# A fused attention and spectral-mixing kernel: product with v moved inside the slot, last tokens of v by pair, constants on other engines

## The chip, the cores and the metric

The kernel runs on one core of a Trainium2 chip. The time is device time in microseconds of one execution; the runs shown are separate executions of the same program. The core has TensorE (in profiles PE, with its weight loads as PEld), VectorE (DVE), ScalarE (ACT), GpSimd (POOL) and SyncE (SP), which here only issues transfers. Each engine works off its own queue in order.

## The reference

Attention over 8 batches and 8 heads, 576 tokens of 64 values, with a causal window of 128 tokens and a linear penalty by distance; then a spectral mixing over the tokens with 64 modes and complex weights, and a residual with a ReLU.

```python
scores = scale * np.matmul(q, k.transpose(0, 1, 3, 2))
rel = pos[:, None] - pos[None, :]
bias = slopes[:, None, None] * (-np.abs(rel).astype(np.float32))[None, :, :]
mask = (rel >= 0) & (rel < window)
...
x = attention output, heads side by side          # (8, 576, 512)
X = np.fft.rfft(x, axis=1)                        # the first 64 modes are used
Yr = einsum('bmd,mde->bme', Xr, w_r) - einsum('bmd,mde->bme', Xi, w_i)
Yi = einsum('bmd,mde->bme', Xr, w_i) + einsum('bmd,mde->bme', Xi, w_r)
y = np.fft.irfft(Y, n=S, axis=1)
u = x + y
return u + np.maximum(u @ w_ch, 0.0)
```

The weights w_r and w_i are 64 matrices of 512 x 512 in float32 each, 134 MB together. Reading them is most of the traffic (163.6 MB are read in all).

## The kernel before

**Units and groups.** A unit is one pair of heads `s` of one batch `b`; there are N = 32. `GROUPS = ((0,), (1, 2, 3))` splits the pairs: units 0 to 7 are pair 0 of the eight batches, units 8 to 31 are pairs 1, 2, 3 of batch 0, then of batch 1, and so on. The rows of the weights that belong to pair 0 can be multiplied as soon as all of group 0 has its spectrum, which happens in the shadow of the attention of group 1. The rows of pairs 1 to 3 need all 32 units.

**Slots.** The instructions of the five engines are laid out by hand (`tc.manual_schedule`): each engine works in the order in which the Python code emits. `_slot(g, n, w0, w1)` (line 603) emits one step of a software pipeline: first half of the scores of unit n (`_score`, line 473), the transposes of q and k of unit n+1 (`_tr`) with their copies out of PSUM by ScalarE (`_evac`), the spectrum of unit n-2 (`_spectrum`, line 564: 5 matmuls for a unit of group 0; for group 1 it does nothing except at the last pair of a batch, where it issues 15), weight tiles of group 0 (`_modes`; one tile is three modes, 24 matmuls), the second half of the scores of unit n, the GpSimd casts of q and k of unit n+2 (`_cast_qk`) and of v of unit n+1 (`_cast_v`), the sorting of v's tokens into tiles of keys (`_keys`, line 432), the product of unit n-1 with v (`_av`, line 521), and a third of the mask product on GpSimd (`_mask3`). The PSUM tiles of scores, of the product with v and of the spectrum have one buffer each.

**Weight tiles in the slots.** From slot 10 on most slots carry one tile of group 0's weights in `w0`; slots whose spectrum has 15 matmuls carry none up to slot 18 and one later. Each tile's load is issued by SyncE at its slot and must wait until the tile three earlier is used: the pool `wpool` has `RING = 3` buffers for each of the tags `wr` and `wi`. All loads share SyncE's one queue, so a load that waits for a buffer holds up every load behind it. At most 8 transfers are under way at a time, since a new one waits for the one eight before it.

**The last 64 tokens of v.** They do not fill a tile of 128 and are handled apart. `_load_vt` (line 379) loads them for all batches and pairs with eight transfers of 128 KB, issued with unit 1, into the first buffers of the `wr` and `wi` rings; VectorE casts them to bfloat16 in two instructions (line 143); `_vt` (line 407) sorts them by a selector matrix `selt` on TensorE, four matmuls of 512 columns for a pair of heads, and VectorE copies the result to `vbt`. Pairs 0 and 3 are done after slot 0, pair 1 after slot 1, pair 2 after slot 2. The tile in PSUM is the single buffer `acc` that `_modes` uses later.

**Constants.** `_consts` (line 238) builds the matrix of the Fourier transform: angles on VectorE, then ScalarE's sine; and the distances for the masks on GpSimd (lines 287 to 295). `_mask` lets ScalarE take the exp of the distances: for pair 0 before slot 0, for pairs 1 to 3 after slot 2. `_select` (line 391) fills the selectors `sel` and `selt` on VectorE.

**Loads of q and k.** They come in batches of units: for group 0 the sizes are 1, 2, 3, 2 units, for group 1 three units each, three buffers in a ring.

After the last slot (n = 35, of which the last four carry no new unit) the weights of group 1 are streamed and multiplied (`_modes` with `last=True`), with the products of x and w_ch in between, and `_finish` makes the output.

Of the kernel before, what the change touches and what calls it, by code (L numbers as in the profile page):

```python
# [16 lines left out]
P = 128  # L17
# [4 lines left out]
ROWS = 3  # L22
# [12 lines left out]
def kernel(  # L35
# [27 lines left out]
    for j, grp in enumerate(GROUPS):  # L63
        mine = [n for n in range(N) if units[n][0] == j]
        sizes = [len(grp)] * B if len(grp) > 1 else [1, 2, 3, 2]
        for m in sizes:
            g.batch[mine[0]], mine = mine[:m], mine[m:]
# [28 lines left out]
    with tc.manual_schedule(engines={ET.SP, ET.PE, ET.Activation, ET.DVE, ET.Pool}):  # L96
        with ExitStack() as wctx:
# [4 lines left out]
            with ExitStack() as actx:  # L102
# [18 lines left out]
                with tc.tile_pool(name="tmpc", bufs=1, side="right") as tp:  # L121
                    for n in range(n0):
# [7 lines left out]
                        if n == 1:  # L130
                            _load_vt(g, tp)
# [9 lines left out]
                    _select(g, tp)  # L141
                    for i, t in enumerate(g.vtf):
                        nc.vector.tensor_copy(
                            g.vtb[:, 4 * i : 4 * i + 4].rearrange("p b c -> p (b c)"),
                            t[:, 0 : 16 * g.D])
                    first = list(dict.fromkeys(u[1] for u in units[:2]))
                    rest = [s for s in range(NP) if s not in first]
                    for s in first:
                        _mask(g, tp, s)
                    for n in range(3):  # L150
                        _slot(g, n, [], [])
                        for s in (first + rest)[n::3]:
                            _vt(g, s, nc.vector.tensor_copy)
                    for s in rest:
                        _mask(g, tp, s)
# [16 lines left out]
                for n in range(3, N + 2 + TAIL):  # L172
# [65 lines left out]
def _consts(g, tp):  # L238
    nc = g.nc
    NM, S, ST = g.NM, g.S, g.ST  # L240
    pi = tp.tile([P, 1], I32)
    nc.gpsimd.iota(pi, [[0, 1]], base=0, channel_multiplier=1)
    mi = tp.tile([P, 2, NM], I32)
    nc.gpsimd.iota(mi, [[0, 2], [1, NM]], base=0, channel_multiplier=0)
# [3 lines left out]
    make_identity(nc, g.ident_b)  # L248
# [3 lines left out]
    pcol = tp.tile([P, 1], FP32)  # L252
    nc.vector.tensor_copy(pcol, pi)
    mrow = tp.tile([P, 2, NM], FP32)
    nc.vector.tensor_copy(mrow, mi)
    scol = tp.tile([P, ST], FP32)
    for st in range(ST):
        nc.vector.tensor_scalar_add(scol[:, st : st + 1], pcol, float(st * P))
    nc.vector.tensor_scalar_add(scol[64:128, 4:5], pcol[64:128], float(4 * P - 64))
    phrow = tp.tile([P, 2, NM], FP32)  # L260
    nc.vector.memset(phrow[:, 0, :], S / 4.0)
    nc.vector.memset(phrow[:, 1, :], S / 2.0)
    MAGIC = float(2**23)
    ang = tp.tile([P, ST * P], FP32)
    for st in range(ST):
        nc.vector.scalar_tensor_tensor(
            out=ang[:, st * P : (st + 1) * P],
            in0=mrow.rearrange("p a b -> p (a b)"),
            scalar=scol[:, st : st + 1], op0=ALU.mult,
            in1=phrow.rearrange("p a b -> p (a b)"), op1=ALU.add,  # L270
        )
    kf = tp.tile([P, ST * P], FP32)
    nc.vector.tensor_scalar_mul(kf, ang, 1.0 / S)
    nc.vector.tensor_scalar(kf, kf, MAGIC, -MAGIC, op0=ALU.add, op1=ALU.add)
    nc.vector.scalar_tensor_tensor(
        out=ang, in0=kf, scalar=-float(S), op0=ALU.mult, in1=ang, op1=ALU.add)
    nc.scalar.activation(
        g.F.rearrange("p a b -> p (a b)"), ang, AF.Sin, scale=2.0 * math.pi / S)
# [4 lines left out]
    eng = nc.gpsimd  # L283
# [3 lines left out]
    eng.tensor_copy(rel, reli)  # L287
    eng.tensor_scalar_add(rel[64:128, 0:256], rel[64:128, 0:256], 127.0)
    eng.tensor_scalar_add(rel[64:128, 256:320], rel[64:128, 256:320], 64.0)
    eng.tensor_scalar(off, rel, 0.0, FAR, op0=ALU.is_lt, op1=ALU.mult)  # L290
    eng.tensor_tensor(out=rel, in0=rel, in1=off, op=ALU.add)
    eng.tensor_scalar(off, rel, float(P), FAR, op0=ALU.is_ge, op1=ALU.mult)
    for a, z, c in ((0, 256, 0), (0, 192, 256), (256, 320, 448)):
        eng.tensor_tensor(
            out=g.rel[:, c : c + z - a], in0=rel[:, a:z], in1=off[:, a:z], op=ALU.add)
    for vb in g.vbs:
        eng.memset(vb[:, :, :, g.D : g.D + 1], 1.0)
    eng.memset(g.vbt[:, :, :, g.D : g.D + 1], 1.0)
    eng.tensor_tensor(
        out=g.ident2, in0=g.ident_b[:, 0:64], in1=g.ident_b[:, 64:128], op=ALU.add)  # L300


def _mask(g, tp, s):
# [75 lines left out]
def _load_vt(g, tp):  # L379


    g.vtb = tp.tile([P, g.B, 4 * g.D], BF16, name="vtb")
    g.vtf = [g.wpool.tile([P, ROWS, g.DM], FP32, tag=tag, name=f"vt{tag}") for tag in ("wr", "wi")]
    g.vtf = [t.rearrange("p a e -> p (a e)") for t in g.vtf]
    for b in range(g.B):
        t = g.vtf[b // 4][:, 256 * (b % 4) : 256 * (b % 4) + 256]
        g.nc.sync.dma_start(
            out=t, in_=g.v[b, :, 512:576, :].rearrange("h (t r) d -> t h (r d)", r=4))


def _select(g, tp):
# [3 lines left out]
    nc.vector.memset(g.sel, 0.0)  # L395
    src = g.ident_b.rearrange("p (i u h) -> p i h u", i=2, h=2)
    for c in range(2):
        nc.vector.tensor_copy(g.sel[:, :, :, c, c::2], src)
# [204 lines left out]
def _slot(g, n, w0, w1):  # L603
# [9 lines left out]
    if 0 <= n - 2 < N:  # L613
        _spectrum(g, n - 2)
# [271 lines left out]
```

## Time and profile before

| | us |
|---|---|
| median of 3 runs | 472.33 |
| the runs | 470.13, 472.33, 472.79 |
| the profiled execution | 470.12 |
| its span, first to last instruction | 468.3 |
| first scores of slot 0, 1, 2, 3 | 7.35, 20.01, 25.41, 29.88 |
| first scores of slot 4, 5, 6, 8 | 35.35, 39.78, 43.97, 52.55 |
| first scores of slot 16, 24, 31 | 90.62, 130.25, 173.45 |
| last spectrum starts | 181.28 |
| last weight tile of group 0 done | 185.4 |

TensorE is busy for 72% of the span, the transfers' 16 engines for 95.3%, VectorE 49%, ScalarE 40%, GpSimd 31%. The shares are means over stages with different limits: attention until about 187 us, the stream of weights until about 430 us, the output after that. A timeline row gives start, duration, engine, line, operation, output and inputs, how many instructions are merged into the row, and in square brackets the idle time before it and what ended it. A row of a stretch gives, for each engine, busy time and instructions, then the granted clock of TensorE (1.00 or 0.50 here), the share of the 16 transfer engines in use, and what they moved in GB/s.

### The profile page before, as it was taken

To read this page: it belongs to the slowest core of one execution; us is meant where nothing else is said; L and a number is where in the kernel's file an instruction comes from. 1 tells how busy PE (TensorE), PEld (TensorE's weight loads), DVE (VectorE), ACT (ScalarE), POOL (GpSimd) and SP (SyncE) were. 2 spreads that over 40 slices of the span, in tenths; PEclk is the share of its full clock that TensorE was granted. 3 is DMA by queue.
4 is the path that set the end of the run, shared out by engine and by line. 5 is a ranking of instruction groups with operands and counts; after the bars stand their busy time and mean duration, and the time that the engine had idled before them with its cause. 6 is when DMAs were issued, how large, how long until landed. Compare 5 with 4: busy or idle time off the path is not lost.

```text
span 468.3 us, 13885 instructions
## 1 busy us (share of the span) xinstructions
PE 337.6 (72%) x5991; PEld 235.5 (50%) x6019; DVE 227.4 (49%) x454; ACT 188.0 (40%) x282; POOL 143.8 (31%) x186
## 2 busy tenths in 40 slices
PE   2788788987889986555666566565664668877994
PEld 1467677766678774333443333343333345634552
DVE  7568776758565564233233233232342334511884
ACT  6487765757555461113222022111220123301783
POOL 8468876759566432000000000000000000000783
PEclk9998997989865597557555565665755759978999
DMA  8999999999979987999999999999999999993687
GB/s 252 294 399 403 347 343 386 383 380 396 395 272 292 349 298 281 421 418 423 402 422 425 423 423 424 422 425 422 423 426 420 426 422 398 420 422 164 233 308 269
DMA packets 60317, 173.92 MB, mean 371 GB/s; under 512 B 4960, under 2 KB 14176, under 8 KB 60256
## 3 DMA queue, kind: packets, MB, share of 16 engines
q1 hardware_dynamic: 60256, 173.03, 95.3%
q8 instruction: 47, 0.77, 0.6%
q14 instruction: 14, 0.11, 0.1%
HBM read 163.58 MB, written 9.44 MB: 369 GB/s over the span
## 4 chain that ended last, share of the span: by engine, by line
DMA 39%; PE 25%; ACT 5%; DVE 4%; issue 3%; SPq 1%; POOL 1%; ACTq 0%; POOLq 0%; DVEq 0%
DMA wi<-in_moe_w_i_dram 38%; PE acc L682 4%; PE acc L678 3%; PE xt L588 2%; PE sc L488 2%; PE vps L444 2%; PE mm L713 2%; PE av L538 2%; PE xw L726 2%; ACT att L502 1%; PE tqk L460 1%; PE zwp L746 1%; PE tp L704 1%; PE y L713 1%; ACT hl L730 1%
## 5 line engine op out<-in xcount | busy, mean ns | idle before, releaser
L730 ACT CAST hl<-xw 64x512 bf16<-64x512 f32 x72 | 41.7, 579 | 165.4 <-PE xw L726 137.4
L682 PEld LDWEIGHTS <-wi 128*128 128x128 bf16 x1024 | 65.8, 105 | 72.6 <-DMA wi<-in_moe_w_i_dram 67.2
L852 POOL TENSOR_TENSOR o<-r,ys 128x512 f32<-128x512 f32 x18 | 22.5, 1273 | 249.9 <-ACT ys L843 249.8
L678 PEld LDWEIGHTS <-wr 128*128 128x128 bf16 x1024 | 69.7, 106 | 43.1 <-DMA wr<-in_moe_w_r_dram 25.6
L682 PE MATMUL acc<-Xlast,wi 128*128 128x16 bf16 x768 | 55.9, 193 | 49.0 <-DMA wi<-in_moe_w_i_dram 49.0
L731 DVE TENSOR_TENSOR hl<-xw,hl 64x512 bf16<-64x512 f32 x72 | 49.6, 689 | 83.3 <-ACT hl L730 83.2
L502 ACT ACTIVATE att<-sc 128x1024 bf16<-128x1024 f32 x64 | 65.5, 1023 | 56.6 <-PE sc L488 31.4
L678 PE MATMUL acc<-Xlast,wr 128*128 128x16 bf16 x768 | 63.0, 194 | 25.0 <-DMA wr<-in_moe_w_r_dram 19.9
L512 DVE TENSOR_TENSOR att<-att,mask 128x1024 bf16<-128x1024 bf16 x64 | 43.6, 683 | 43.4 <-ACT att L502 42.9
L517 POOL TENSOR_TENSOR att<-att,mask 128x512 bf16<-128x512 bf16 x32 | 44.5, 1390 | 51.1 <-ACT att L502 51.1
L726 PE MATMUL xw<-wch,xT 128*128 128x512 bf16 x121 | 54.0, 573 | 4.9 <-issue 3.1
L706 DVE COPY xT<-tp 128x512 bf16<-128x512 bf16 x36 | 15.2, 423 | 58.4 <-PE tp L704 58.2
L468 ACT COPY qkT<-tqk 128x576 bf16<-128x576 bf16 x62 | 39.3, 634 | 0.3 <-PE tqk L460 0.2
L460 PE MATMUL tqk<-ident_b,qkb 64*64 64x64 bf16 x1152 | 30.5, 209 | 9.9 <-ACT qkb L422 4.4
L488 PE MATMUL sc<-qkT,qkT 64*64 64x256 bf16 (+1 forms) x512 | 30.6, 313 | 9.6 <-ACT qkT L468 4.1
L460 PEld LDWEIGHTS <-qkb 64*64 64x64 bf16 x1152 | 30.2, 125 | 11.2 <-ACT qkb L422 4.6
L726 PEld LDWEIGHTS <-xT 128*128 128x128 bf16 x144 | 19.1, 138 | 22.3 <-issue 20.2
L444 PE MATMUL vps<-vc,sel 128*64 128x128 bf16 x512 | 25.5, 254 | 1.8 <-issue 0.7
L429 POOL CAST vc<-v 128x512 bf16<-128x512 f32 x32 | 26.1, 815 | 0.9 <-PE sc L497 0.9
L538 PE MATMUL av<-vb,att 128*128 128x65 bf16 x448 | 23.0, 211 | 0.6 <-DVE x L558 0.6
L555 DVE TENSOR_TENSOR x_sb<-av,rec 128x512 bf16<-128x512 f32 x32 | 22.1, 692 | 0.6
L678 PE MATMUL acc<-X,wr 128*128 128x16 bf16 x256 | 19.1, 193 | 4.2 <-ACT ZTa L691 4.2
(119 smaller groups left out, 526.8 us busy)
## 6 DMA issues: line engine op xcount, KB each, us to landing
wr<-in_moe_w_r_dram SPq DMA_DIRECT2D x85, 768.0 KB, 8.3
wi<-in_moe_w_i_dram SPq DMA_DIRECT2D x85, 768.0 KB, 9.7
v<-in_v_dram SPq DMA_DIRECT2D x64, 128.0 KB, 7.3
out_dram<-o SPq DMA_DIRECT2D x32, 256.0 KB, 2.3
q<-in_q_dram SPq DMA_DIRECT2D x9, 864.0 KB, 9.1
k<-in_k_dram SPq DMA_DIRECT2D x9, 864.0 KB, 10.1
q<-in_q_dram SPq DMA_DIRECT2D x2, 576.0 KB, 6.1
k<-in_k_dram SPq DMA_DIRECT2D x2, 576.0 KB, 7.3
```

The costliest lines, as they stand in the source:

```text
L444: g.nc.tensor.matmul(o[64 * r : 64 * r + 64, i, h], lhsT=g.sel[:, i, h, c], rhs=v[:, 2 * c + r], start=(c == 0), stop=(c == 1), tile_posit ...
L460: g.nc.tensor.transpose(tp[hs, r, :], u.b[w][hs, r], g.ident_b[hs, hs], tile_position=(64 * hh, 64 * hh))
L468: (copy or g.nc.scalar.copy)(dst.rearrange("c (p r) -> c p r", r=g.R), u.tp[w].rearrange("c r p -> c p r"))
L488: nc.tensor.matmul(sc[64 * r : 64 * r + 64, hh, c0 : c0 + nq], lhsT=kT[hs, kt * P + r : kt * P + P : 2], rhs=qT[hs, kt * P : kt * P + nq], ...
L502: nc.scalar.activation(a.rearrange("p h c -> p (h c)"), sc.rearrange("p h c -> p (h c)"), AF.Exp, scale=1.0 / math.sqrt(g.D))
L512: nc.vector.tensor_tensor(out=a, in0=a, in1=m, op=ALU.mult)
L517: g.nc.gpsimd.tensor_tensor(out=a, in0=a, in1=g.mask[:, g.units[n][1], :, 256:512], op=ALU.mult)
L678: nc.tensor.matmul(o, lhsT=wr[:, a].bitcast(BF16)[:, 1::2][:, c], rhs=X[:, a, 1:3, :, m], start=(a == 0), stop=False)
L682: nc.tensor.matmul(o, lhsT=wi[:, a].bitcast(BF16)[:, 1::2][:, c], rhs=X[:, a, 0:2, :, m], start=False, stop=(a == A - 1))
L726: nc.tensor.matmul(xw, lhsT=xT[:, dt], rhs=g.wch[:, dt], start=(dt == 0 and g.way[n] != "q"), stop=(dt == 3))
L730: nc.scalar.copy(g.hl[hi, n, h], xw[hi])
L731: nc.vector.tensor_tensor(out=g.hl[lo, n, h], in0=xw[hi], in1=g.hl[hi, n, h], op=ALU.subtract)
```

## The change

Six edits go together.

1. In `_slot` the product with v (`_av` of unit n-1) and the spectrum (of unit n-2) change places: the product now stands between the transposes and the second scores, the spectrum behind the keys.
2. The last tokens of v are loaded and sorted pair by pair. Pair 0 is loaded with unit 0 (two transfers of 128 KB) into a tile of its own; pairs 1 to 3 with six transfers ahead of the first weight tile, into one buffer of the `wr` ring. GpSimd casts one pair at a time, and TensorE sorts it with 64 matmuls of 64 columns (by batch, quarter and head of the pair). Pair 0 is done after slot 0, pairs 1, 2, 3 after slots 3, 4, 5, each with its mask ahead of it on ScalarE.
3. The distances are computed on VectorE, in place of GpSimd, with fewer instructions.
4. The chain of angles on VectorE is shorter.
5. The selectors are filled by GpSimd in place of VectorE.
6. The batches of q and k for group 0 are 1, 2, 2, 3 units.

```diff
-        sizes = [len(grp)] * B if len(grp) > 1 else [1, 2, 3, 2]
+        sizes = [len(grp)] * B if len(grp) > 1 else [1, 2, 2, 3]
...
-                        if n == 1:
-                            _load_vt(g, tp)
+                        if n == 0:
+                            for s in GROUPS[0]:
+                                _load_vt(g, s, tp.tile([P, 2, 4 * g.D], FP32, name=f"vtf{s}"))
+                        if n == g.first[1] - 1:
+                            t = g.wpool.tile([P, ROWS, DM], FP32, tag="wr", name="vtf")
+                            for i, s in enumerate(GROUPS[1]):
+                                _load_vt(g, s, t[:, i].rearrange("p (h c) -> p h c", h=2))
...
-                    _select(g, tp)
-                    for i, t in enumerate(g.vtf):
-                        nc.vector.tensor_copy(
-                            g.vtb[:, 4 * i : 4 * i + 4].rearrange("p b c -> p (b c)"),
-                            t[:, 0 : 16 * g.D])
...
+                    for s in GROUPS[0]:
+                        _mask(g, s)
+                    _select(g)
+                    todo_s = [(0, s) for s in GROUPS[0]] + [(3 + i, s) for i, s in enumerate(GROUPS[1])]
+                    for n in range(g.first[1] - 1):
                         _slot(g, n, [], [])
-                        for s in (first + rest)[n::3]:
-                            _vt(g, s, nc.vector.tensor_copy)
-                    for s in rest:
-                        _mask(g, tp, s)
+                        for k, s in todo_s:
+                            if k == n:
+                                if s not in GROUPS[0]:
+                                    _mask(g, s)
+                                _vt(g, tp, s)
...
+    prod = tp.tile([P, ST, NM], FP32)
+    nc.vector.tensor_tensor(
+        out=prod, in0=scol.unsqueeze(2).broadcast_to([P, ST, NM]),
+        in1=mrow.unsqueeze(1).broadcast_to([P, ST, NM]), op=ALU.mult)
+    ang = tp.tile([P, ST, 2, NM], FP32)
+    for ri in range(2):
+        nc.vector.tensor_scalar_add(ang[:, :, ri], prod, S / (4.0 - 2 * ri))
...
+    nc.vector.tensor_scalar(kf, ang, 1.0 / S, MAGIC, op0=ALU.mult, op1=ALU.add)
+    nc.vector.tensor_scalar(kf, kf, -MAGIC, -float(S), op0=ALU.add, op1=ALU.mult)
+    nc.vector.tensor_tensor(out=ang, in0=ang, in1=kf, op=ALU.add)
...
+    nc.vector.tensor_copy(rel[0:64], reli[0:64])
+    nc.vector.tensor_scalar_add(rel[64:128, 0:256], reli[64:128, 0:256], 127.0)
+    nc.vector.tensor_scalar_add(rel[64:128, 256:320], reli[64:128, 256:320], 64.0)
+    nc.vector.tensor_scalar(off, rel, 1.0 - P, FAR, op0=ALU.add, op1=ALU.mult)
+    nc.vector.scalar_tensor_tensor(
+        out=rel, in0=rel, scalar=-FAR, op0=ALU.mult, in1=rel, op1=ALU.max)
     for a, z, c in ((0, 256, 0), (0, 192, 256), (256, 320, 448)):
-        eng.tensor_tensor(
-            out=g.rel[:, c : c + z - a], in0=rel[:, a:z], in1=off[:, a:z], op=ALU.add)
+        nc.vector.tensor_tensor(
+            out=g.rel[:, c : c + z - a], in0=rel[:, a:z], in1=off[:, a:z], op=ALU.max)
...
+    g.selt = tp.tile([P, g.B, 4, 64], BF16, name="selt")
+    nc.gpsimd.memset(g.sel, 0.0)
+    nc.gpsimd.memset(g.selt, 0.0)
...
-def _load_vt(g, tp):
+def _load_vt(g, s, t):
+    for hh in range(2):
         g.nc.sync.dma_start(
-            out=t, in_=g.v[b, :, 512:576, :].rearrange("h (t r) d -> t h (r d)", r=4))
+            out=t[:, hh], in_=g.v[:, 2 * s + hh, 512:576, :].rearrange("b (t r) d -> t b (r d)", r=4))
+    g.unit["vt", s] = t
...
+def _select(g):
+    nc = g.nc
     src = g.ident_b.rearrange("p (i u h) -> p i h u", i=2, h=2)
     for c in range(2):
+        nc.gpsimd.tensor_copy(g.sel[:, :, :, c, c::2], src)
+    src = g.ident_b.rearrange("p (t b) -> p b t", b=g.B)
     for r in range(4):
+        nc.gpsimd.tensor_copy(g.selt[:, :, r, r::4], src)
...
+def _vt(g, tp, s):
+    nc = g.nc
+    v = tp.tile([P, 2, 4, g.D], BF16, tag="vtb", bufs=2, name=f"vtb{s}")
+    nc.gpsimd.tensor_copy(v.rearrange("p h r d -> p h (r d)"), g.unit.pop(("vt", s)))
     acc = g.mpsum.tile([P, 4, 2, MB, 8], FP32, tag="acc", name="vtp")
...
-    for r in range(4):
-        g.nc.tensor.matmul(acc, lhsT=g.selt[:, s, r], rhs=v[:, r], start=(r == 0), stop=(r == 3))
-    copy(g.vbt[:, s, :, 0 : g.D], acc)
+    for b in range(g.B):
+        for r in range(4):
+            _pair(nc, acc[:, b], [g.selt[:, b, r]] * 2, [v[:, h, r] for h in range(2)],
+                  start=(r == 0), stop=(r == 3))
+    nc.vector.tensor_copy(g.vbt[:, s, :, 0 : g.D], acc)
...
         _tr(g, n + 1, 1)
-    if 0 <= n - 2 < N:
-        _spectrum(g, n - 2)
+    if 0 <= n - 1 < N:
+        _av(g, n - 1)
     for w in w0:
         _modes(g, *w)
...
         _keys(g, n)
-    if 0 <= n - 1 < N:
-        _av(g, n - 1)
+    if 0 <= n - 2 < N:
+        _spectrum(g, n - 2)
     if n < N:
         _mask3(g, n)
```

`_pair` (line 710, unchanged) issues two matmuls that fill the two halves of the output's partitions.

## The prediction

> **What bounds it now.** First the page: the slices (11.7 us each) and the chain of waits.
>
> ```profile
> span 468.3 us, 13885 instructions
> ...
> PEclk9998997989865597557555565665755759978999
> DMA  8999999999979987999999999999999999993687
> ...
> DMA 39%; PE 25%; ACT 5%; DVE 4%; issue 3%; SPq 1%; POOL 1%; ACTq 0%; POOLq 0%; DVEq 0%
> ```
>
> From slice 17 on (187 us) the transfers are full and the chain is almost all "wi": the three-pair weights are streamed, and nothing here touches that stream. It can begin only when the last spectrum is done and ring buffers come free. So the time is the end of the attention part (0 to 187 us) plus 283 us that stay, and I only ask how that end moves. Second, the timeline of an ordinary slot (slot 5):
>
> ```profile
> 39.78 0.41 PE L488 MATMUL sc<-qkT,qkT 64*64 64x256 bf16 x8 [0.28 <-ACT qkT L468]
> 40.02 0.76 PE L460 MATMUL tqk<-ident_b,qkb 64*64 64x64 bf16 x36
> 41.36 0.40 PE L588 MATMUL xt<-F,x_sb 128*128 128x128 bf16 x4 [0.58 <-DVE x_sb L555]
> ...
> 41.84 0.39 PE L488 MATMUL sc<-qkT,qkT 64*64 64x256 bf16 x8
> ...
> 42.19 0.64 PE L444 MATMUL vps<-vc,sel 128*64 128x128 bf16 x16
> 42.76 0.60 PE L538 MATMUL av<-vb,att 128*128 128x65 bf16 x14
> ```
>
> ScalarE and GpSimd in the same slot:
>
> ```profile
> 42.37 1.02 ACT L502 ACTIVATE att<-sc 128x1024 bf16<-128x1024 f32 x1 [0.57 <-POOL qkb L422]
> 43.28 0.63 ACT L468 COPY qkT<-tqk 128x576 bf16<-128x576 bf16 x1
> ```
> ```profile
> 43.47 1.39 POOL L517 TENSOR_TENSOR att<-att,mask 128x512 bf16<-128x512 bf16 x1 [0.57 <-ACT att L502]
> ```
>
> The next slot's first scores start at 43.97, when ScalarE's second copy is done. So a slot is what lies before the second scores (41.84 - 39.78 = 2.06) plus a tail of 2.13 (exp, copy, hand-overs). TensorE work behind the second scores is hidden while it fits in the tail: there keys and av take 1.5. Third, the first slot, where the next slot waits for the last tokens of v:
>
> ```profile
> 14.49 1.58 POOL L517 TENSOR_TENSOR att<-att,mask 128x512 bf16<-128x512 bf16 x1
> ...
> 15.12 1.87 PE L413 MATMUL vtp<-vtb,selt 128*128 128x512 bf16 x4 [1.23 <-DVE vtb L143]
> ...
> 20.01 0.64 PE L488 MATMUL sc<-qkT,qkT 64*64 64x256 bf16 x8
> ```
>
> Fourth, the stretches around a change of clock and around the hand-over to the stream (PE, PEld, DVE, ACT, POOL busy; clock; DMA share; GB/s):
>
> ```profile
> 75.11:78.53 3.42, 2.18 (x78) 1.93 (x80) 2.88 (x7) 2.34 (x4) 3.42 (x4) 1.00 1.04 401
> 78.53:81.94 3.41, 3.41 (x74) 2.91 (x68) 1.74 (x5) 1.81 (x3) 1.90 (x3) 0.50 1.08 370
> ```
> ```profile
> 182.00:184.00 2.00, 2.00 (x26) 1.33 (x26) 0.33 (x1) 0.00 (x0) 0.00 (x0) 0.50 0.29 111
> 184.00:186.00 2.00, 1.84 (x52) 1.58 (x48) 0.56 (x3) 0.54 (x1) 0.44 (x4) 0.50 0.25 52
> ```
>
> **The change, part by part.** *Start.* Angles on VectorE: today 1.00 to 5.96; by halves of the 640-wide rows (0.49 to 0.82) the new chain ends near 4.6, yet the sine starts at 6.43 because ScalarE is casting q and k until 5.12 and then loads its table (1.28): worth nothing. Distances (GpSimd 2.05 to 9.77 today) cost VectorE some 2.5 us, by rows of 0.2 to 0.8: done at 7.2. That pushes the two copies of the transposes to 8.6 (7.29 today) and lets the masks start at about 8.5, behind ScalarE's table, not 9.80: the first exp comes 1.3 us sooner. But GpSimd now does the selectors: two memsets (VectorE's rows 0.27 and 0.91), six strided copies (VectorE 0.43 to 0.49 for 128 elements, GpSimd 0.21 for 32, so 0.25 to 0.5 each), and then the rest of its queue: four casts of q and k (0.66), two of v (0.61), the product of 1.4 to 1.6, and only then the cast of the last tokens. From k of unit 1 landing (10.1 today, two transfers of 0.64 us issue later now) this adds to about 17.7. Then 64 matmuls of 64 columns, which the trace does not have: nearest is L444 (64 weight columns, paired column halves), 1.07/16 = 67 ns at half clock and 0.64/16 = 40 at full; L460 (36 in 0.74) gives 21 as the low end. At 55 ns, 3.5: the second slot starts at 21.0, **+1.0** (-1.1 to +2.6).
>
> *Slots 1 to 3* lose a vt product each in slots 1 and 2 and six mask activations (3.23 us) ahead of slot 3: 5.40, 4.47, 5.47 become about 5.2, 4.1, 4.2: **-1.9** (-2.5 to -1).
>
> *Last tokens pair by pair.* In slots 3, 4 and 5 TensorE's queue holds 64 matmuls between this slot and the next one's scores, waiting for a GpSimd cast that stands behind the mask product of the same slot. From the second scores on: 0.53, exp 1.02, product 1.39, cast 0.61, hand-overs 0.1, 64 x 40 ns = 2.5: 6.15 in place of 2.13, so 4.0 x 3 = **+12.0** (with 21 ns 8.5, with 67 ns 17.5). The masks of these pairs (1.1 on ScalarE) hide in that wait. Were the cast not late, matmuls right behind keys and spectrum would cost 3 x 1.8. Behind the waiting matmuls stands all of TensorE's next slot, and for that ScalarE and VectorE.
>
> *Transfers.* The three pairs' v takes a buffer of the wr ring until the cast of slot 5. The third weight tile waits for it (today issued at 33.87), SyncE with it, and behind it v of unit 7 and q, k of 11. By the sums above SyncE moves on near 52; v then lands some 5 us later, while slot 6's cast needs it at 56 and the mask product queues behind: **+2** (0 to +6). Regrouping q and k 2-2-3 lets units 3 and 4 land sooner; the 4.35 us that GpSimd waits for q at 20.43 lay under the vt matmuls: 0.
>
> *Order in the slot.* av (0.92) stands where the spectrum stood. Slots 3 to 9: 0.92 replaces 0.56 + 0.58 wait, -0.2 each, -1.4. In slots 12 to 30 a spectrum of 15 matmuls (1.58, wait 0.5) stands in every third slot: -1.1 there, less where the clock is halved and TensorE binds: -5 over seven. In the thirteen others with weight tiles (0.8) av comes on top: loops of 3.9 (slot 16, 90.62 to 94.52) become 4.8; seven such at +0.9, six bound by TensorE at +0.35, two without tiles +0.3: +9. Sum **+2.6** (0 to +8). At the end the last av no longer waits behind weight tiles, nor these behind the last spectrum, so a ring buffer comes free before 182: of the hole in the transfers, 2 x (1 - 0.28) + 2 x (1 - 0.24) = 3.0 us (shares against the full 1.05), **-3** (-3.4 to 0).
>
> *Clock.* With av gone from the tail TensorE idles there: 2.13 less the 0.35 and 0.57 of second scores and keys (steps of the starts above) is 1.2 us a slot. The stretch with 2.18 of 3.42 busy was followed by half clock. Between 24 and 181 us 14 of 46 stretches are halved; a halved one costs 3.41 x (1 - 0.64/1.07) = 1.37 where TensorE binds (L444's two rates), about half elsewhere. Eight more at 0.65: **+5** (-5 if half of the fourteen go, +20 if all 46 are halved).
> The Trainium skill ("TensorE: Matmul & The Clock Gate", Part 1) has the clock halved after an idle window of about 3.4 us. By that rule gaps of 1.2 us halve nothing more and the sum would be 483; the rows above, with no idle window before 78.53, speak against it.
>
> Sum: 1.0 - 1.9 + 12.0 + 2 + 2.6 - 3 + 5 = +17.7 on the profiled execution's own 470.1 (span 468.3 and 1.8 around it): **488**. That execution is the lowest of those shown, 0.5% under their median, within the noise.
>
> **Rivals.** (a) The clock stays as today, +5 becomes 0: 483; with matmuls at L460's rate too (8.5 for 12.0) 479.5. For it: in 37 to 68 us slots with idle stretches of 0.6 kept full clock; against: the gaps get twice as long, and the selector's 64 columns fill all 128 rows, as L444's do. (b) Half clock through slots 8 to 31: 488 + 15 = 503. For it: 133 to 164 us was halved without a break. (c) The other side: the transfers set the attention part. In 20 to 130 us their share is 1.0 and more, and v of unit 8 was cast (50.99) only as it landed. If the held-up third tile leaves enough in flight (landing takes 9 us), waits in slots 3 to 5 go into slack and 12 + 2 vanish, with the clock term: 469, 0.7% under the median; 460 if av on top costs nothing either and of the order only the 6.4 gained stand. It decides if SyncE is held for less than those 9 us; I get some 25. (d) The edits cancel: 8.5 in slots 3 to 5 against -1.1, -2.5, -3.4 and nothing else: 472.
>
> **Numbers.** Forecast 0.55, (a) 0.20, (b) 0.12, (c) 0.08, (d) 0.05. All but (c) and (d) are slower: 0.87; same (within 0.5%, about what a measurement can tell) 0.05; faster 0.08. Range 471 to 500: (c) lies below it and (b) above.
>
> **What would show it.** Scores of slot 6 near 54 to 56 (43.97 today); in slots 3 to 5 vt matmuls waiting for GpSimd, 2 us or more; the third wr tile issued near 52; a hole in the transfers before it; av ahead of the second scores and 4.8 us loops at full clock; more halved stretches; no hole at the hand-over. Wrong: vt matmuls starting right behind the spectrum, slot 6 before 48, or transfers full throughout.

## The result and the profile after

| | before | after |
|---|---|---|
| median of 4 runs, us | 471.23 | 493.38 |
| the runs | 468.09, 470.13, 472.33, 472.79 | 486.97, 493.0, 493.75, 493.94 |
| the profiled execution | 470.12 | 486.97 |
| mean granted TensorE clock of the runs | 0.755 (profiled) | 0.749 (profiled), 0.707, 0.721, 0.721 |

The kernel after takes 1.045 of the time before (95% interval 1.034 to 1.055): slower. The profiled execution of the kernel after is its shortest by 6 us, and the one with the highest clock; the steps below are read from it (16.9 us over the profiled execution before), and the other 5 us of the 22 between the medians lie in executions without a trace. Comparisons with an interval leave out runs more than 1.5% above the lowest of their kernel; where a median over all runs says something else, both stand, and e1 has no interval, since only two of its four runs are left.

The page of the kernel after, in its slices of 12.1 us, and its chain of waits:

```profile
span 485.2 us, 14375 instructions
...
PEclk9997979765896589655667556557555759988999
DMA  7992799999997799999899999999999999995587
GB/s 246 338 367 91 263 374 316 388 369 325 371 397 278 242 365 316 319 421 422 354 423 422 423 422 427 422 424 423 424 423 422 427 422 416 421 423 234 217 320 246
...
DMA 51%; PE 21%; issue 10%; POOL 7%; ACT 4%; SPq 3%; DVE 3%; POOLq 0%; DVEq 0%; ACTq 0%
```

Two things are new against the page before: the fourth slice has the transfers at 2 tenths (91 GB/s), and the chain has "POOL 7%" and "issue 10%" where it had 1% and 3%. The first scores of each slot, which are the slots' starts:

| first scores of slot | 1 | 3 | 4 | 5 | 6 | 7 | 8 | 12 | 16 | 24 | last spectrum |
|---|---|---|---|---|---|---|---|---|---|---|---|
| before | 20.01 | 29.88 | 35.35 | 39.78 | 43.97 | 47.96 | 52.55 | 70.31 | 90.62 | 130.25 | 181.28 |
| after | 20.57 | 29.57 | 36.67 | 45.03 | 52.07 | 55.83 | 64.33 | 83.85 | 106.55 | 146.82 | 198.71 |
| later by | 0.6 | -0.3 | 1.3 | 5.3 | 8.1 | 7.9 | 11.8 | 13.5 | 15.9 | 16.6 | 17.4 |

So the loss is made in two places: 8.4 us in slots 3 to 5 and 3.9 in slot 7; then 5.7 more, a little at a time, up to the last spectrum. Slot 4 in the timeline (start, duration, engine, line, operation, output and inputs, count, and in brackets the idle time before it and what ended it; clock half of full from 43.2 us on):

```profile
40.09 1.02 ACT L495 ACTIVATE att<-sc 128x1024 bf16<-128x1024 f32 x1 [1.16 <-issue]
...
41.19 1.39 POOL L510 TENSOR_TENSOR att<-att,mask 128x512 bf16<-128x512 bf16 x1 [3.92 <-ACT att L495]
...
42.53 0.60 POOL L400 CAST vtb<-vtf 128x512 bf16<-128x512 f32 x1
...
43.18 1.91 PE L706 MATMUL vtp<-vtb,selt 128*64 128x64 bf16 x64 [1.37 <-POOL vtb L400]
...
45.02 0.19 PEld L481 LDWEIGHTS <-qkT 64*64 64x64 bf16 x8
45.03 0.64 PE L481 MATMUL sc<-qkT,qkT 64*64 64x256 bf16 x8
```

Read from the bottom: the next slot's scores start when the 64 vt matmuls are out of the way; those waited for the cast; the cast stood in GpSimd's queue behind the mask product; and that waited for the exp of the second scores. This is the chain that the prediction drew. Slot 7 has the same engine late for another reason:

```profile
55.83 0.41 PE L481 MATMUL sc<-qkT,qkT 64*64 64x256 bf16 x8 [0.57 <-ACT qkT L461]
...
59.62 0.61 POOL L422 CAST vc<-v 128x512 bf16<-128x512 f32 x1 [7.52 <-DMA v<-in_v_dram]
60.20 1.15 POOL L510 TENSOR_TENSOR att<-att,mask 128x512 bf16<-128x512 bf16 x1
...
61.40 0.34 PE L531 MATMUL av<-vb,att 128*128 128x65 bf16 x3 [3.61 <-POOL att L510]
```

v of unit 7 was issued behind the third weight tile, at 51.9 us, and landed at 59.5. GpSimd's mask product of slot 6 queues behind its cast, and the product with v, which now stands ahead of slot 7's second scores, waits 3.61 us for that mask product.

An ordinary slot later on: slot 11 of the kernel after in the timeline, then its window, then that of slot 10 before, which has the same work (columns of a window: us, busy time with instruction counts of PE, PEld, DVE, ACT, POOL; clock; DMA share; GB/s):

```profile
79.07 0.41 PE L481 MATMUL sc<-qkT,qkT 64*64 64x256 bf16 x8 [1.14 <-ACT qkT L461]
79.31 0.76 PE L453 MATMUL tqk<-ident_b,qkb 64*64 64x64 bf16 x36
80.00 0.60 PE L531 MATMUL av<-vb,att 128*128 128x65 bf16 x14
...
81.72 0.39 PE L481 MATMUL sc<-qkT,qkT 64*64 64x256 bf16 x8
...
82.06 0.64 PE L437 MATMUL vps<-vc,sel 128*64 128x128 bf16 x16
83.85 0.41 PE L481 MATMUL sc<-qkT,qkT 64*64 64x256 bf16 x8 [1.15 <-ACT qkT L461]
```
```profile
79.07:83.85 4.78, 3.63 (x115) 3.16 (x115) 3.19 (x8) 3.11 (x4) 3.63 (x5) 1.00 1.04 356
```
```profile
60.85:64.77 3.92, 3.63 (x114) 3.15 (x115) 3.18 (x8) 3.11 (x4) 3.63 (x5) 1.00 1.03 356
```

All five engines do the same work at the same clock, but the slot lasts 4.78 instead of 3.92: the 0.9 us of av have gone from the tail, where TensorE now idles 1.15 us, to the stretch ahead of the second scores, on which ScalarE's exp and with it the next slot wait.

### The profile page after: what moved, and what is told of

Read it like the earlier page. It is cut to its first block, busy times and chain, and to the rows that moved or that the text cites. A ratio compares the mean times of both kernels' runs of the same rounds, so it can differ in the third digit from the quotient of the medians.

```text
span 485.2 us, 14375 instructions
## 1 busy us (share of the span) xinstructions
PE 343.5 (71%) x6259; PEld 241.2 (50%) x6259; DVE 228.1 (47%) x443; ACT 188.2 (39%) x282; POOL 144.3 (30%) x189
## 4 chain that ended last, share of the span: by engine, by line
DMA 51%; PE 21%; issue 10%; POOL 7%; ACT 4%; SPq 3%; DVE 3%; POOLq 0%; DVEq 0%; ACTq 0%
DMA wi<-in_moe_w_i_dram 40%; DMA k<-in_k_dram 5%; PE acc L675 4%; POOL qkb L415 3%; PE acc L671 3%; DMA v<-in_v_dram 3%; DMA q<-in_q_dram 2%; POOL vc L422 2%; PE sc L481 2%; PE av L531 2%; PE tqk L453 1%; PE xw L719 1%; PE mm L706 1%; PE xt L581 1%; PE tp L697 1%
## 5 line engine op out<-in xcount | busy, mean ns | idle before, releaser
L845 POOL TENSOR_TENSOR o<-r,ys 128x512 f32<-128x512 f32 x18 | 22.5, 1274 | 248.1 <-DVE r L837 246.3
L505 DVE TENSOR_TENSOR att<-att,mask 128x1024 bf16<-128x1024 bf16 x64 | 45.2, 707 | 48.0 <-ACT att L495 47.5
L719 PE MATMUL xw<-wch,xT 128*128 128x512 bf16 x144 | 61.5, 574 | 0.0
L510 POOL TENSOR_TENSOR att<-att,mask 128x512 bf16<-128x512 bf16 x32 | 43.0, 1345 | 59.8 <-ACT att L495 56.8
L453 PE MATMUL tqk<-ident_b,qkb 64*64 64x64 bf16 x1152 | 31.9, 215 | 7.9 <-ACT qkb L415 4.5
L453 PEld LDWEIGHTS <-qkb 64*64 64x64 bf16 x1152 | 31.3, 131 | 9.4 <-ACT qkb L415 4.5
L422 POOL CAST vc<-v 128x512 bf16<-128x512 f32 x32 | 27.8, 868 | 9.9 <-DMA v<-in_v_dram 9.8
L481 PEld LDWEIGHTS <-qkT 64*64 64x64 bf16 x512 | 10.8, 118 | 24.8 <-ACT qkT L461 18.6
L415 POOL CAST qkb<-q 128x576 bf16<-128x576 f32 x31 | 21.5, 694 | 5.2 <-DMA q<-in_q_dram 5.2
```

What stands on the lines that cost most here:

```text
L422: g.nc.gpsimd.tensor_copy(u.vc, u.v)
L453: g.nc.tensor.transpose(tp[hs, r, :], u.b[w][hs, r], g.ident_b[hs, hs], tile_position=(64 * hh, 64 * hh))
L481: nc.tensor.matmul(sc[64 * r : 64 * r + 64, hh, c0 : c0 + nq], lhsT=kT[hs, kt * P + r : kt * P + P : 2], rhs=qT[hs, kt * P : kt * P + nq], ...
L505: nc.vector.tensor_tensor(out=a, in0=a, in1=m, op=ALU.mult)
L510: g.nc.gpsimd.tensor_tensor(out=a, in0=a, in1=g.mask[:, g.units[n][1], :, 256:512], op=ALU.mult)
L719: nc.tensor.matmul(xw, lhsT=xT[:, dt], rhs=g.wch[:, dt], start=(dt == 0 and g.way[n] != "q"), stop=(dt == 3))
```

## The experiments

Twelve kernels were run. "Clock" is the mean granted TensorE clock over all runs of a kernel; the last column is the clock between 24 and 190 us, about the attention part, of the profiled execution (0.83 before, 0.80 after; up to the last spectrum alone it is 0.85 and 0.81).

| | median us | before beside it | ratio (95%) | clock | 24 to 190 |
|---|---|---|---|---|---|
| e1 own tile | 490.2 | 471.7 | - | 0.720 | |
| e2 cast early | 487.9 | 471.7 | 1.043 (1.034 to 1.053) | 0.728 | |
| e3 order back | 480.2 | 471.7 | 1.028 (1.019 to 1.036) | 0.753 | |
| e4 vt back | 483.3 | 471.7 | 1.035 (1.024 to 1.045) | 0.721 | |
| e5 order alone | 482.2 | 470.9 | 1.018 (1.008 to 1.027) | 0.722 | 0.79 |
| e6 vt alone | 478.4 | 470.9 | 1.019 (1.014 to 1.025) | 0.751 | |
| e7 constants alone | 471.0 | 470.9 | 1.001 (0.998 to 1.005) | 0.764 | |
| e8 order, keys twice | 479.8 | 470.9 | 1.022 (1.016 to 1.027) | 0.756 | 0.90 |
| e9 order, filler | 477.1 | 471.5 | 1.011 (1.006 to 1.016) | 0.760 | 0.89 |
| e10 before, filler | 469.9 | 471.5 | 0.999 (0.995 to 1.003) | 0.767 | |
| e11 spectrum in the tail | 468.2 | 471.5 | 0.993 (0.989 to 0.996) | 0.758 | |
| e12 the same, pairs 1 to 3 | 469.6 | 469.3 | 0.999 (0.995 to 1.002) | 0.753 | |

### Is the hole in the transfers a price of its own? (e1)

The trace after suggested a second account beside the prediction's: transfers idle from 41 to 54 us, and by bytes moved the kernel is 13.7 us late at 54 us, which alone would explain most of the 16.9. In these windows the share of the transfers is 0.02:

```profile
41.00:45.00 4.00, 2.30 (x68) 2.12 (x67) 1.22 (x3) 1.69 (x4) 3.72 (x5) 0.78 0.02 4
45.00:49.00 4.00, 3.79 (x98) 3.22 (x96) 2.60 (x7) 2.71 (x4) 0.05 (x1) 0.79 0.02 4
```

```diff
...                                                       # _consts ahead of the loads of unit 7 on
-  t = g.wpool.tile([P, ROWS, DM], FP32, tag="wr", name="vtf")
-  for i, s in enumerate(GROUPS[1]):
-      _load_vt(g, s, t[:, i].rearrange(...))
+  for tag, s in zip(("kf", "ang", "rel"), GROUPS[1]):      # space of the constants
+      t = tp.tile([P, 640], FP32, tag=tag, name=f"vtf{s}")
+      _load_vt(g, s, t[:, 0:512].rearrange("p (h c) -> p h c", h=2))
```

> The kernel after, with the last tokens of pairs 1 to 3 loaded into space of their own (freed by the angles and distances) instead of a buffer of the wr ring; casts and matmuls stay where they are. Both theories: the third weight tile is issued near 31 to 34 us instead of 50.9, and the hole in the transfers at 41 to 54 goes; TensorE still waits for the casts in slots 3 to 5 (8.4 us more in these three slots than in the kernel before). Theory A (TensorE's waits set the end, as the prediction summed them): only slot 7's extra 3.9 us comes back, with half a clock stretch or so: median 493 becomes 488 to 490. Theory B (the transfers set the end; the kernel after is late by the hole, about 13.7 us of transfers): slots 3 to 5 still last 7 to 8 us each, but the slots behind catch up, because the transfers were their limit: 474 to 480.

The third tile was issued at 34.3 us and the transfers stayed full until 58, as both theories had it. The median fell by 3.2 us only (493.4 to 490.2; the runs, 483.8 to 492.1, overlap with those of the kernel after), which fits theory A and is far from theory B. The hole did not vanish; it moved to where SyncE next has to wait for a buffer that the late slots still hold (9.5 us for one that a GpSimd cast of q or k frees):

```profile
48.00:54.00 6.00, 3.55 (x78) 2.94 (x79) 3.07 (x8) 2.60 (x4) 3.11 (x4) 0.54 1.06 371
60.00:66.00 6.00, 5.29 (x171) 4.37 (x165) 4.24 (x10) 4.66 (x6) 5.70 (x7) 1.00 0.01 4
```

By bytes moved, e1 is only 0.3 us behind the kernel before at 54 us, and 12.2 at 84, where the kernel after is 13.5 behind. So a hole in the transfers is here a sign that consumption is late, not a cost of its own. Theory B falls. What slot 7 won was in part lost again in slots 3 to 5 (25.1 us for 22.5): TensorE stood still for 1.84 and 2.87 us in slots 4 and 5 with nothing to wait for ("issue"), see the last section.

### The casts out of the way (e2)

```diff
   _slot(g, n, [], [])
+  if n in (0, 2):
+      for s in GROUPS[n > 0]:
+          _cast_vt(g, tp, s)            # GpSimd cast of the pair's last tokens
   for k, s in todo_s:
       ...
           _vt(g, tp, s)                 # now the 64 matmuls and the copy alone
```

> The kernel after, with the three casts of the last tokens of pairs 1 to 3 put into GpSimd's queue at the end of slot 2 (their loads land by 27.9 us); the ring buffer and the matmuls stay where they are. The vt matmuls then start right behind the spectrum, 1.2 to 1.9 us a slot, and the ring buffer comes free near 32 instead of 51. Both theories: slots 3 to 5 last 5.5 to 6 us, no hole in the transfers. Theory A: 3 x 1.8 of the 8.4 us in slots 3 to 5 stay and slot 7's wait goes, so 493 - (8.4 - 4) - 3.9 = about 485, less with the clock: 480 to 485. Theory B: 472 to 477, as in the run with a tile of its own or lower.

487.9: above what either theory gave. The transfers stay full until 54 us, then fall to shares of 0.5 to 0.6 until 72, where no hole was expected. Slots 3 to 5 lasted 6.1, 7.6 and 7.5 us, although the matmuls no longer wait for a cast (in slot 4 they follow the spectrum at 41.53). In slot 4 the time went into a stop in the middle of the spectrum, of 2.36 us:

```profile
38.39 0.23 PE L595 MATMUL xt<-F,x_sb 128*128 128x128 bf16 x1
40.98 0.40 PE L595 MATMUL xt<-F,x_sb 128*128 128x128 bf16 x3 [2.36 <-issue]
41.32 0.28 PE L595 MATMUL xt<-F,x 64*128 64x128 bf16 x1
41.53 1.92 PE L720 MATMUL vtp<-vtb,selt 128*64 128x64 bf16 x64
```

So the late cast was one part of the price of the pair-by-pair way, and its 64 matmuls (1.9 us) with the stops of TensorE in these slots another.

### The two large edits, each undone and each alone (e3 to e7)

```diff
# e3 on the kernel after; e5 is the reverse on the kernel before
-    if 0 <= n - 1 < N:
-        _av(g, n - 1)
+    if 0 <= n - 2 < N:
+        _spectrum(g, n - 2)
...
-    if 0 <= n - 2 < N:
-        _spectrum(g, n - 2)
+    if 0 <= n - 1 < N:
+        _av(g, n - 1)
# e4 on the kernel after; e6 is the reverse on the kernel before, its selectors on VectorE
-    _load_vt(g, s, ...); _vt(g, tp, s) after slots 0, 3, 4, 5
+    _load_vt(g, tp) with unit 1; two casts on VectorE; _vt(g, s, nc.vector.tensor_copy) after slots 0, 1, 2
# e7 on the kernel before: _consts and the filling of the selectors as in the kernel after
-    nc.vector.tensor_copy(dst[:, :, :, :, r], src)
+    nc.gpsimd.tensor_copy(dst[:, :, :, :, r], src)
```

> The kernel after, with the product with v back behind the keys and the spectrum back between the transposes and the second scores; all else as in the kernel after. The prediction's terms for it (order +2.6, hand-over -3, clock +5) give 493 - 4.6 = 488 to 489. Theory B (transfers late by the hole, the slots behind it have slack): 493 within 2 us, or up to 3 slower by the hole at the hand-over.

> The kernel after, with the last tokens loaded, cast and multiplied as in the kernel before (batch by batch, at the start, three products of 512 columns in slots 0 to 2 and the fourth with the first); new constants, new batches of q and k and the new order stay. Both theories: slots 3 to 5 and the hole in the transfers as in the kernel before, so 14 us and more come back: 493 becomes 479 or less. What stays over 471 is the price of order, clock and constants: the prediction's 2.6 - 3 + 5 gives 474 to 476; if the order costs nothing because the transfers are the limit: 469 to 472.

> The kernel before, with only the order in the slot changed: product with v between the transposes and the second scores, spectrum behind the keys. By the prediction's terms (order +2.6, hand-over -3, clock +5) 471 becomes 475 to 477. By what putting the order back gave (493.4 to 480.2) it costs some 13: 482 to 486. If the two halves of the change only hurt together (the product ahead of the second scores waits behind GpSimd's late mask product in the slots with last tokens), 471 to 474. In each case the mean granted clock of the runs says how much of it is clock: near 0.76 (as before) the slots themselves are longer, near 0.72 (as in most runs of the kernel after) the clock is part of it.

> The kernel before, with only the last tokens of v loaded by head, cast on GpSimd in slots 0 and 3 to 5 and placed by 64 matmuls of 64 columns a pair (selectors made on VectorE, masks pair by pair; old constants, old batches, old order). By the prediction's terms (+12 in slots 3 to 5, +2 transfers, -1.9 in slots 1 to 3, start +1) 471 becomes 482 to 485; by what the old way gave inside the new kernel (493.4 to 483.3) 480 to 482; if the kernel after pays for the casts mostly by the new place of the product with v, 473 to 476.

> The kernel before, with only the new angles, the distances on VectorE and the selectors on GpSimd (of the shape of the kernel before: 512 columns a pair). The selectors' strided copies (0.5 us each and more, with a memset of 2048 elements) now stand in GpSimd's queue ahead of the masks' product of slot 0; in the kernel after with the old way of the last tokens slot 1 began at 23.7 instead of 20.0. So slot 1 1 to 4 us later and 471 becomes 471 to 475; if the transfers of the first weight tiles set the attention part, no change (471 within 1).

| | in the kernel after | in the kernel before | the prediction's terms |
|---|---|---|---|
| order in the slot | 13.2 by medians (493.4 to 480.2), 8.0 by the ratios | 11.3 by medians, 8.4 by the ratio | 2.6 - 3 + 5 = 4.6 |
| last tokens pair by pair | 10.1 by medians (493.4 to 483.3), 4.7 by the ratios | 7.5 by medians, 9.1 by the ratio | 12 + 2 + 1 - 1.9 = 13.1 |
| constants | - | 0.1 | in the +1 |

The order cost two to three times what was predicted, the last tokens less. Undoing the order (e3) gave more than either theory allowed, so theory B is refuted a second time, and the prediction's sum for the order with it. e4 stays above its limit of 479 too: with the old way of the last tokens the kernel is by medians where the order alone is (483.3 and 482.2), while the profiled executions differ by 4.1 (481.7 and 477.6), 3.7 of it in the first slot. e5 fits by its median what e3 gave, with a clock of 0.722, and lies at 479 by its ratio; e6 lies between its expectations. In the profiled executions the two edits also cost more together: from slot 3 to slot 8 the kernel before takes 22.7 us, the order alone 24.0, the last tokens alone 30.5, the kernel after 34.8, so 3 more than the sum of both. The rows of slot 7 above show one way: the late mask product holds the product with v, and in the new order everything in the slot stands behind that product.

The constants cost nothing in the end: in e7 slot 1 starts at 20.9 instead of 20.0, and the last spectrum at 181.4 against 181.3.

### Clock or path? (e8 to e10)

e5's executions are spread over 11 us with the clock: 475.1 and 477.6 at 0.739 and 0.738, 481.6 to 485.8 at 0.704 to 0.726. If TensorE's idle 1.15 us in the tail is what lowers the clock, filling it should raise it.

```diff
# e8, in _keys
+ again = n > 8 and g.units[n - 2][1] != 3       # slots without a spectrum
- for i in range(2):
+ for _ in range(2 if again else 1):
+   for i in range(2):
# e9 (order alone) with 6, e10 (before) with 4, at the end of _slot
+ if 12 < n < N and g.units[n - 2][1] != 3:
+     for _ in range(FILL):
+         g.nc.tensor.matmul(g.fill, lhsT=g.ident_b, rhs=g.ident_b, start=True, stop=True)
```

> The kernel before with only the order in the slot changed, and in the slots from the ninth on that have no spectrum the sixteen matmuls of the keys done twice over (the same result written again): 0.64 us more of TensorE work at full clock, in the gap behind the second scores where TensorE waits for ScalarE. If the clock is what the new order costs (idle gaps in the tail keep it halved), the mean granted clock is 0.02 or more above that of the order alone and the time 3 us or more below it. If the slots are longer because the product with v lies ahead of the second scores, clock or not, the time is that of the order alone, or up to 5 us above it where the extra matmuls end behind the tail.

> The kernel before with only the order in the slot changed, and at the end of each slot without a spectrum, from slot 13 on, six matmuls of 128 columns into an unused part of the spectrum's bank: 0.6 us of TensorE work by the spectrum's row (4 in 0.40) in the gap of some 1.2 us before the next first scores, that nobody waits for. If half clock in the gaps is the main price of the order, the mean granted clock is 0.75 or more and the time 474 to 477 (482 for the order alone); if the path is (the product with v ahead of the second scores, 0.9 us a slot), the clock rises and the time stays at 480 to 484.

> The kernel before, its order kept, with four such matmuls (0.4 us) at the end of each slot without a spectrum from slot 13 on. If half clock costs what the spread of the runs suggests (0.3 us for each us at half clock; 43 of 56.9 such us lie between 120 and 190 us), and the filler lies in gaps, 471 becomes 464 to 469; if TensorE sets these slots' length, the 0.4 us come on top in some 13 slots: 472 to 476.

The attention part of e5 and of e9 as one window each:

```profile
24.00:190.00 166.00, 139.19 (x3328) 113.84 (x3327) 109.80 (x238) 99.34 (x132) 105.77 (x118) 0.79 0.95 340
```
```profile
24.00:190.00 166.00, 136.83 (x3395) 110.86 (x3394) 110.90 (x236) 99.79 (x133) 104.94 (x118) 0.89 0.93 337
```

The clock does what was expected of it: 0.756 and 0.760 over the runs of e8 and e9, as in the profiled execution before (0.755), and 0.10 more in the attention part. The time follows only in part. e8, whose extra matmuls delay VectorE's copy of the keys as well, is 2.4 us below the order alone by the median, short of the 3 that was asked of the clock theory, and 1.7 above it by the ratios. e9 (run on another chip than e5 and e8, as were e10 to e12) comes out at the upper edge of what was expected if the clock is the main price: its runs lie between 474.1 and 479.8, so the long executions of e5 are gone and the median is 5 us lower (3.5 by the ratios, whose intervals overlap). But the two profiled executions take the same (477.4 and 477.6) with 0.10/0.5 x 166 = 33 us less at half clock in this window (some 10 of them before slot 13 at 77.1 us, where the two kernels are still the same), and the last spectrum of e9 starts at 189.8, not before e5's 186.7. And in the kernel before the filler (e10) changes nothing. So the half-clocked stretches go with the spread of the order alone and a few us of its median; for the kernel after this is inferred from its clock. What is left with the clock restored, 5 us (1.011, 1.006 to 1.016), is the path, with what the filler itself may cost. How the 0 to 5 us of the clock split between gain and the filler's own 0.6 us a slot stays open.

### Half of the order (e11, e12)

```diff
# e11, in _slot, on the kernel before
-    if 0 <= n - 2 < N:
-        _spectrum(g, n - 2)
...
         _keys(g, n)
+    if 0 <= n - 2 < N:
+        _spectrum(g, n - 2)
     if 0 <= n - 1 < N:
         _av(g, n - 1)
```

> The kernel before, with the spectrum alone moved behind the keys, and the product with v left behind it: the half of the new order that takes TensorE work out from ahead of the second scores without putting the product with v there. By the prediction's steps slots 3 to 9 lose 0.56 + 0.58 ahead of the second scores and their tail (0.57 + 0.64 + 0.6 + 0.92 = 2.7) is 0.6 longer than ScalarE's 2.13; the seven later slots with a spectrum lose 1.58 + 0.5 and gain about 1.6: 7 x 0.5 + 7 x 0.5 = 7 off at most, so 464 to 468 if the product with v ahead of the second scores is what the new order pays for. If instead the late spectrum (x_sb read a slot's half later, tiles of weights behind it) is the price, 473 to 482 as with the whole order.

468.2, 0.993 (0.989 to 0.996): a little better than both kernels, and the direction of the path theory: the spectrum may leave the stretch ahead of the second scores, the product with v should not enter it. The gain, 3.3 us, is half of the 7 that were worked out as the most. In the first units nothing is gained (slots 3 to 7 take 22.9 us, 22.7 before), because the second scores then wait for the first exp, which still holds their bank:

```profile
41.48 1.02 ACT L502 ACTIVATE att<-sc 128x1024 bf16<-128x1024 f32 x1 [0.71 <-PE sc L488]
...
42.55 0.39 PE L488 MATMUL sc<-qkT,qkT 64*64 64x256 bf16 x8 [0.55 <-ACT att L502]
```

> The kernel before, with the spectrum behind the keys (and ahead of the product with v) for the units of pairs 1 to 3 only, whose spectrum has fifteen matmuls in every third slot; the first eight units keep it ahead of the second scores. With the spectrum late for all units the eighth slot began 1.1 us later and the ninth 2.0 later than before, and the last spectrum 2.3 sooner. If those two belong to the first units, the time is 1 to 2 us below that run: 465 to 468, 0.98 to 0.995 of the kernel before. If the early lateness is only the spread between executions, 467 to 470, as with the spectrum late for all.

e12 moves the spectrum of the units of pairs 1 to 3 alone (the first diff's two conditions become `n - 2 < g.first[1]` and `g.first[1] <= n - 2`). The time is in the second range, but the kernel before took 469.3 beside it: no gain, where the later slots are those of e11 and should have kept its gain. So e11's 0.7% is a measured difference without a shown cause; it is the only version here that beats both kernels.

## Why the prediction was right, and where its steps were not

The total was near (488, and 486.97 in the profiled execution; 493.4 in the median, inside the range), the direction right, and the main chain as drawn. But its terms were off in opposite directions and cancelled: by the single edits the order was put too low (4.6 for 8 to 13) and the last tokens too high (13.1 for 5 to 10). That the sum came within 1 us of the profiled execution is in part luck. Step by step, profiled executions against each other:

| step | predicted | measured | from |
|---|---|---|---|
| start | +1.0 | +0.6 | slot 1's first scores |
| slots 1 and 2, and masks | -1.9 | -0.9 | slot 3 at 29.57 for 29.88 |
| last tokens, slots 3 to 5 | +12.0 | +8.4 | 22.5 us for 14.1 |
| transfers, slots 6 and 7 | +2 | +3.7 | 12.3 for 8.6 |
| order and clock, slots 8 to the last spectrum | +2.6 + 5 | +5.7 | 134.4 for 128.7 |
| hand-over to the stream | -3 | -0.6 | 288.3 for 288.8 to the end |
| sum | +17.7 | +16.9 | 486.97 - 470.12 |

- **The last tokens.** The mechanism was right: the vt matmuls wait for the cast in all three slots (2.16, 1.37 and 2.15 us), slot 6 starts at 52.07 (predicted 54 to 56). The size was off through the price of one matmul: 55 ns in the first slot and 40 in the others were taken from the keys' row; the trace has 1.91/64 = 30 ns in slot 4, at half clock, and 1.20/64 = 19 ns in slot 5, at full clock:

```profile
50.94 1.20 PE L706 MATMUL vtp<-vtb,selt 128*64 128x64 bf16 x64 [2.15 <-POOL vtb L400]
```

  The keys' matmul has 128 columns to move, these have 64; the low end, from the transposes of 64 columns (21 ns), was the row to take.
- **The transfers.** SyncE moved on at 50.9 (predicted 52), v of unit 7 landed at 59.5. The step was mis-sized at 2: what waits in slot 7 is no longer the keys only but the product with v ahead of the second scores, for 3.61 us. With the old order (e3) the same late v holds the keys for 2.11.
- **The order.** This was the step that failed most. Loops of 3.9 became 4.8, as predicted. But the seven slots with fifteen spectrum matmuls were to win 5 and won 2.0 (44.3 to 42.3 us together; 42.4 with the order alone); the sixteen others lost 7.4 (76.5 to 84.0; 83.9 with the order alone). The -1.4 of slots 3 to 9 did not come: with the order alone the slots from 3 up to 8 take 1.3 us more, and e11 shows that taking the spectrum out there wins nothing, as the second scores then wait for the exp. Slots 8 to 30 take 5.4 us more in both kernels with the new order (126.3 for 120.9). Alone, the order costs 8 to 11 us, not 4.6.
- **The hand-over.** The hole is filled, as the share shows (0.29 and 0.25 before), but the end came only 0.6 us sooner after the last spectrum:

```profile
198.00:200.00 2.00, 2.00 (x39) 1.49 (x36) 0.00 (x0) 0.00 (x0) 0.00 (x0) 0.50 0.81 285
200.00:202.00 2.00, 1.62 (x23) 1.10 (x23) 0.82 (x2) 0.00 (x0) 0.00 (x0) 0.50 0.93 326
```

  The share was read as work done; at a share near 1 the stream moves 425 GB/s later on, and 285 to 337 from 198 to 206 us. The weight transfer issued at 185.36 before and at 202.42 after, the same one in the order of issue, landed 9.0 us after the end of the last spectrum in both kernels.
- **The clock.** Eight more halved stretches were predicted. From 24 us to the last spectrum the clock is 0.85 before and 0.81 after:

```profile
24.00:181.28 157.28, 134.25 (x3301) 109.52 (x3298) 106.48 (x240) 99.07 (x132) 102.02 (x118) 0.85 1.00 358
```
```profile
24.00:198.71 174.71, 139.44 (x3503) 116.00 (x3500) 110.44 (x239) 100.39 (x133) 105.61 (x121) 0.81 0.90 319
```

  That is (1 - 0.85)/0.5 x 157.3 = 47 and (1 - 0.81)/0.5 x 174.7 = 66 us at half clock, some 14 and 19 stretches: five to six more, 3.6 us at the predicted 0.65 each. What a stretch costs is not shown: e9 beside e5 had much less half clock for the same profiled time. The other executions of the kernel after (0.707 to 0.721 over the run, for 0.749) take 6 us more; that they had more halved stretches in this part fits their clock but is not shown, as they have no trace. That half clock needs no long idle time is shown by e5: the longest idle time of TensorE in its attention part is 1.8 us, at a clock of 0.79. That work in the gaps raises the clock is shown by the runs: 0.704 to 0.739 in e5, 0.737 to 0.771 in e8 on the same chip, 0.751 to 0.777 in e9. The rule of the Trainium skill that the prediction weighed ("TensorE: Matmul & The Clock Gate", Part 1) asks for an idle window of about 3.4 us; by it e5's clock would not fall in this part. The same page's section "A second HAM failure mode: psum-queue depth-cycling", which has short idles make the clock swing, agrees with e5's 0.79 at idle times of 1.8 us and less.
- **The start.** The masks did start sooner (8.86 for 9.80), but the first exp, which was to come 1.3 us sooner, came at 10.90 for 10.86: VectorE's copies of the transposes ended at 10.15, not 8.6, for a reason given in the last section. Slot 1 began 0.6 later, within the term.
- **The rivals.** (c), that the transfers set the attention part, is refuted by e1, whose transfers ran full until 58 us for a gain of 3.2 at most. (a) and (b) are about the clock: the profiled execution (487.0, five to six more halved stretches) lies between (a) and the forecast, the median (493.4) between the forecast and (b). (d), that the edits cancel, falls with the measured loss of 17 to 22 us.

## What to carry to other kernels

Moving work out of a stage's tail into its head cost its full length here (0.9 us a slot) though every engine's sum stayed the same, so count for every moved instruction who stands behind it at the new place, and which late engine it makes the whole slot wait for. A hole in the transfers may be only the shadow of late consumption: give the transfer its own buffer, and if the hole moves and the time stays, look at the consumer. And a total that comes out right says little about its terms; undoing each edit and making it alone took four runs and showed that two were off by some 3 to 9 us each.

## What the runs showed of the hardware

**TensorE's instructions seem to arrive in blocks, and short matmuls to outrun them.** The page counts 47 transfers on queue 8, of kind "instruction", before and 49 after, for 12010 and 12518 instructions of PE and PEld: one for about every 255. In e2 one of these transfers, of 16 KB, starts at 38.8 us, takes 1.0 us, and TensorE, which had stopped at 38.62, goes on at 40.98. The next starts at 44.7, with a stop from 45.55 to 47.17. In the stretch from 38 to 41 us the ordinary transfers are full:

```profile
DMA packets 690, 1.18 MB, mean 395 GB/s; under 512 B 42, under 2 KB 202, under 8 KB 688
...
q1 hardware_dynamic: 688, 1.16, 103.4%
q8 instruction: 1, 0.02, 2.1%
```

In the attention part such blocks come about every six us before and after; in e1 and e2 the stops of 1.6 to 2.9 us lie in the slots that have 64 short matmuls with their weight loads, where the longest before the change is 1.1 in the slots. That the stop is the block's arrival is read from the times only; it was not tried by changing the code's length alone.

**VectorE stood still beside a memset on GpSimd.** The new chain of angles lost 1.4 us to it:

```profile
2.24 0.88 DVE L264 TENSOR_SCALAR ang<-prod 128x320 f32<-128x320 f32 x2
3.15 1.89 DVE L267 TENSOR_SCALAR kf<-ang 128x640 f32<-128x640 f32 x1
5.08 0.49 DVE L268 TENSOR_SCALAR kf<-kf 128x640 f32<-128x640 f32 x1
```
```profile
2.90 1.80 POOL L296 MEMSET selt<- 128x2048 bf16 x1
```

Two instructions of one form take 1.89 and 0.49 us; the first lies across the memset of the selector (2.90 to 4.70) and ends 0.34 us after it. The same 1.89 and 0.49 stand in e1 to e4 and in e7, which all have this memset; in the kernel before, without it, the first instruction takes 0.49 as well, beside a TENSOR_SCALAR of GpSimd (3.97 to 5.61), so not every GpSimd instruction does this. The Trainium skill ("SBUF — State Buffer", section "SBUF: two separate sides") has GpSimd and VectorE, the latter in modes that use two ports, share one pair of ports that the one that starts first holds for its whole instruction while the other is blocked; the rows of 1.89 us agree with it, but no run here shows the mode of the instruction. So the selectors' move to GpSimd took back what the shorter chain of angles had gained: it ends at 6.43 us, where the prediction had 4.6 and the kernel before has 5.96.
